# Last pair pass of an attention and expert kernel: second product as seven block products of scaled float16 parts

## The chip, the cores and the metric

The kernel runs on one core of a Trainium2 chip. The metric is the device time of one execution in microseconds (us); the time of a kernel is the median of its runs. The engines are named as in the profile: PE (TensorE, matmuls), PEld (its weight loads), DVE (VectorE), ACT (ScalarE), POOL (GpSimd) and SP (SyncE, which issues every DMA of this kernel).

## The reference

The input is attention (4 batches, 8 heads, 768 positions, 64 features a head) and four experts that every token passes through. Cut to what matters:

```python
# attention: each query sees its neighbours within 16 positions and 24 block summaries
scores_all = concat([where(|i - j| < 16, scale * q @ k.T, -1e9), scale * q @ k_sum.T + log(32)])
a = softmax(scores_all)                        # k_sum: max over blocks of 32
x = a @ concat([v, v_sum])                     # v_sum: mean over blocks of 32; 3072 tokens x 512
# four experts, all of them for every token
p = domain_probs / (domain_probs.sum(-1) + 1e-9)
out = sum over e of p[:, e] * (relu(x @ w1[e]) @ w2[e])   # w1: 512 x 1024, w2: 1024 x 512
```

## The kernel before

The 3072 tokens are eight blocks of 384 (TB, three tiles of 128 tokens each). Attention is done in pieces of 96 queries (`psc` scores, `ms` masked scores, `aw` weights, `awT` the weights turned by a DMA, `px` the values). It feeds the experts, and its pieces stand between the expert products by a table of due times (`steps`, lines 915 to 940, called from `advance`).

The plan of the experts (line 955) has three first passes over single blocks and then three **pair passes** (`PAIRS`, line 778). Pair pass 1 does blocks 2 and 3, pass 2 blocks 4 and 5, pass 3 blocks 6 and 7, each with all four experts, in the orders (3, 2, 1, 0), (0, 1, 2, 3) and (3, 2, 1, 0). Attention is finished in the course of pass 2.

An expert in a pair pass (`pair_units`, lines 857 to 912) has two products. The **first product**, relu(x @ w1), takes the 1024 hidden features in four blocks i of 256. For a pair of token blocks this is a product of 2x2 blocks, and it is made with seven block products in place of eight (`SEVEN`, line 851; `m` counts them from 0): sums and differences of blocks of x and w1 are multiplied into PSUM banks `pha` to `phd`. ACT copies bank a to b after m = 0 and bank d to a buffer `p5` after m = 1; DVE adds these to make banks c (after m = 2) and d (after m = 4). Values are kept as two parts, a rounded one (hi) and the rest (lo), both of type fp32r, and each product is hi·hi + hi·lo + lo·hi: per block i there are 7 x 6 matmuls of 128x384. `to_h` (line 747) makes the hidden values from PSUM: relu and rounding on ACT (`hh`), the rest on DVE (`hl`).

The **second product**, h @ w2, is `mm2` (lines 752 to 776), called by `second` (line 799): per token tile 8 feature blocks x 3 matmuls of 128x512 into a bank `po`, which DVE multiplies by the expert's share `pw` of each token and adds to `acc` (lines 770 to 773). After the fourth expert `acc` goes out. `w2` in two parts is made once and kept in memory (`wd`); later passes load it again, 512 KB for each of 8 feature blocks (`weights`, line 683). The operands of the first product, `w1s` and `w`, are made from `wr` (the raw load of w1 or w2) in the first pass that needs them, by `w1_operands` (line 707), and are loaded again later. `setup_v` (line 168) loads a block of v in four chunks `vch` and makes its means.

What runs when is settled while the program is built: the builder takes instructions in the order of the code, with priorities (RUSH = 200 for the small steps between block products), and an estimate of times places each on its engine's queue. From then on every engine works through its own queue in order, and an instruction waits there for its operands and for buffers to come free. `wr` has 4 buffers, `w1` 14, `w2` 8, `hh` and `hl` 16 each, and PSUM 2 banks `sc`, 2 `av` and 4 `mm`. An instruction recorded by the helper has its line 75, so the profile's rows are told apart by names and shapes.

Of the kernel before, what the change touches and what calls it, by code (L numbers as in the profile page):

```python
# [25 lines left out]
G = 4  # L26
# [36 lines left out]
def attn_moe(ctx: ExitStack, tc: tile.TileContext, qvL, qv0, v0L, kD, kT, vT, w1L, w2L, dpL, cst, out):  # L63
# [82 lines left out]
    def block_stats(ch, dst, hp, op):  # L146
        V.tensor_reduce(dst[:, hp, :], ch.rearrange("p (n k) -> p n k", k=BLK), axis=AX.X, op=op)
# [19 lines left out]

    def setup_v(b):
        vsr = sb.tile([P, G, NB], F32, name=f"vsr{b}", tag="vsr")
        for hp in range(H // 2):  # L170
            ch = chunk(f"vch{b}_{hp}")
            load_chunk(b, hp, ch, vT)
            block_stats(ch, vsr, hp, ALU.add)
        stack_v(b, vsr)

    def stack_v(b, vsr):
        vs5 = sb.tile([P, G, 5, NB], F32, name=f"vs5_{b}", tag="chunk", bufs=CHUNKS)
# [524 lines left out]

    WS = ("11", "s2", "s1", "s3", "12", "s4", "22")

    def w1_operands(e, pr):
        ws = {w: w1_part(f"w1{w}{e}_{pr}") for w in WS}
        if (e, pr) in stored:
            for w in WS:  # L710
                SP.dma_start(ws[w].bitcast(F32), stored[e, pr][w])
            return ws
        r1, r2 = (load_weights(w1L, e, 2 * pr + j, "1") for j in range(2))
        a11, a12 = r1[:, 0:256], r1[:, 256:512]
        a21, a22 = r2[:, 0:256], r2[:, 256:512]
        stored[e, pr] = {}

        def parts(w, raw, lo):
# [33 lines left out]
    def mm2(tb, e, ts, hT, w2):  # L752
        po = {t: ps_mm.tile([P, 512], F32, name=f"po{tb}_{e}_{t}", tag="mm") for t in ts}
        done = 0
        for m, (fc, (whi, wlo)) in enumerate(w2.items()):
            for t in ts:
                hh, hl = (x[:, t * P : (t + 1) * P] for x in hT[tb, fc])
                PE.matmul(po[t], hh, whi, start=m == 0, stop=False)
                PE.matmul(po[t], hh, wlo, start=False, stop=False)
                PE.matmul(po[t], hl, whi, start=False, stop=m == FC - 1)  # L760
                done += 3 * US2
            if m < FC - 1 and (len(ts) > 1 or m in (2, 5)):
                yield done, 1.0
                done = 0
        for t in ts:
            gt = tb * (TB // P) + t
            pe = pw[:, gt, e : e + 1]
            added[gt] = added.get(gt, 0) + 1
            if added[gt] == 1:
                acc[gt] = sb.tile([P, DM], F32, name=f"acc{gt}", tag="acc", bufs=6)  # L770
                V.tensor_scalar_mul(acc[gt], po[t], pe)
            else:
                V.scalar_tensor_tensor(acc[gt], po[t], pe, acc[gt], op0=ALU.mult, op1=ALU.add)
            if added[gt] == E:
                SP.dma_start(out[gt * P : (gt + 1) * P, :], acc.pop(gt))
# [28 lines left out]
        for tb in tbs[len(whole) :]:  # L804
            yield from mm2(tb, e, range(TB // P), hT, w2)

    def with_fetch(units):
        for n, us in enumerate(units):
            if n in (1, 8):
                fetch()  # L810
            yield us

    def plain_units(tbs, e, early=0, last=False):
# [40 lines left out]
        ("b", "s3", "t3"), ("c", "s4", "22"), ("b", "22", "t4"),  # L854
    )

    def pair_units(pr, e, last=False):

        tbs = (2 * pr, 2 * pr + 1)
        xp = xpair[pr]  # L860
        hT = {}
        _, w2 = kept.pop(e, ({}, {}))
        kept.clear()
        order = orders[pr, e]
        for n, i in enumerate(order):
            fetch((pr, e, i))
# [10 lines left out]
            for m, (k, w, x) in enumerate(SEVEN):  # L877
# [11 lines left out]
                if m == 0:  # L889
                    A.copy(new("b"), o)  # L890
                elif m == 1:
                    five = sb.tile([P, TB], F32, name=f"p5{pr}_{e}_{i}", tag="hs", bufs=2)
# [10 lines left out]
                else:  # L903
                    to_h(hT, tbs[0], e, f2, o)
                ahead_of.close()
                if m == 3:
                    for fc in (f1, f2):
                        if fc not in w2:
                            w2[fc] = weights(w2L, e, fc, "2", PL)
                yield 6 * US1, SLOW  # L910
        kept[e] = {}, w2
        yield from with_fetch(second(tbs, e, hT, w2, last))


    steps = []
# [130 lines left out]
```

## Time and profile before

| | us |
|---|---|
| median of 3 runs | 1179.01 (1178.67 to 1179.54) |
| the profiled execution | 1176.52 |
| its span | 1174.7 |
| PE busy in 0 to 276 (first passes) | 262.37 of 276 |
| DVE busy in 0 to 276 | 186.56 of 276 |

The profile comes from one execution, whose own time is 1176.52; the span is the time from the first to the last recorded instruction in it. Busy times are sums over the instructions of one engine. PSUM and weight traffic apart, an engine of the five that is idle while PE is busy costs nothing, so the profile is read from PE's side: where PE waits, for whom, and what that engine did just before.

### The profile page before, as it was taken

Reading aid. Unit: us, or ns where it says so; the run is one execution under the profiler, and the core shown is the slowest. Engines: PE = TensorE matmul, PEld = TensorE weight load, DVE = VectorE, ACT = ScalarE, POOL = GpSimd, SP = SyncE. Lnnn points to the kernel's source line nnn. Section 1 sums busy time; section 2 is a strip of 40 time slices with the busy share of each in tenths; the row PEclk is TensorE's granted clock in tenths of the full one; section 3 lists DMA queues with packets and bytes.
Section 4 is the critical chain, followed back from the end, with each engine's and each line's share of the span. In section 5 each row is a group of like instructions: output and inputs, shape, how many; then the busy total and the mean of one; then the engine's idle time right before and its main releaser. Section 6 shows DMA issues by size and latency. Waiting matters only on the chain.

```text
span 1174.7 us, 20612 instructions
## 1 busy us (share of the span) xinstructions
PE 1150.5 (98%) x7188; PEld 1021.0 (87%) x7188; DVE 631.4 (54%) x1519; ACT 541.2 (46%) x1586; POOL 468.5 (40%) x578
## 2 busy tenths in 40 slices
PE   9898899999979999999999999999999999999998
PEld 7787789998968989898898989889898998989896
DVE  6778775555796837558586543535354222323131
ACT  5678667655666736546375443434343211202020
POOL 2398677846786737547265122221202000000000
PEclk9999999999999999999999999999999999999999
DMA  6699787957996878789963859678571556566531
GB/s 240 227 281 321 225 250 218 305 118 215 307 251 182 272 228 263 225 277 288 320 196 102 255 149 289 202 213 284 141 205 61 159 156 212 165 197 189 163 98 54
DMA packets 202329, 249.66 MB, mean 213 GB/s; under 512 B 82672, under 2 KB 118512, under 8 KB 202224
## 3 DMA queue, kind: packets, MB, share of 16 engines
q1 hardware_dynamic: 202224, 248.34, 69.6%
q8 instruction: 57, 0.93, 0.3%
q14 instruction: 48, 0.39, 0.1%
HBM read 174.22 MB, written 57.15 MB: 197 GB/s over the span
## 4 chain that ended last, share of the span: by engine, by line
PE 85%; DMA 4%; DVE 4%; POOL 3%; ACT 2%; issue 1%; SPq 1%; POOLq 0%; DVEq 0%; ACTq 0%
PE po L75 42%; PE phb L75 13%; PE pha L75 9%; PE ph L75 5%; PE phd L75 4%; PE phc L75 4%; PE psc L75 4%; PE px L75 3%; DMA vch<-in_vT 1%; PE pav L75 1%; DMA wr<-in_w2L 1%; DMA kch<-in_kT 1%; DVE ms L75 1%; SPq L75 1%; ACT ms L75 1%
## 5 line engine op out<-in xcount | busy, mean ns | idle before, releaser
L75 PE MATMUL po<-w,hh 128*128 128x512 f32 x1536 | 480.5, 394 | 0.0
L75 PEld LDWEIGHTS po<-w,hh 128*128 128x128 f32 x1536 | 284.2, 188 | 61.0
L75 PE MATMUL po<-w,hl 128*128 128x512 f32 x768 | 302.8, 397 | 0.0
L75 PEld LDWEIGHTS po<-w,hl 128*128 128x128 f32 x768 | 144.4, 188 | 31.5
L75 POOL TENSOR_TENSOR ks<-kr,ks 128x304 fp32r<-128x304 f32 x112 | 99.7, 897 | 176.8 <-ACT ks L75 160.5
L75 DVE CUSTOM_DVE_ANT_0 ms<-psc,c_sb 96x152 f32<-96x152 f32 x256 | 69.2, 306 | 104.6 <-PE psc L75 103.4
L75 PE MATMUL phb<-xh_t,w1s 128*128 128x384 f32 x384 | 114.2, 338 | 0.1
L75 ACT ACTIVATE ms<-ms,nb 96x152 f32<-96x152 f32 x256 | 104.3, 415 | 16.5 <-DVE nb L75 15.6
L75 PE MATMUL pha<-xh,w 128*128 128x384 f32 x384 | 110.7, 335 | 0.0
L75 DVE SCALAR_TENSOR_TENSOR acc<-po,pw,acc 128x512 f32<-128x512 f32 x72 | 51.9, 746 | 108.8 <-PE po L75 108.8
L75 PE MATMUL ph<-xh,wh 128*128 128x384 f32 x256 | 88.0, 347 | 4.8 <-ACT wh L75 3.7
L75 PE MATMUL ph<-xl,wh 128*128 128x384 f32 x256 | 87.4, 341 | 2.3 <-DVE xl L75 2.3
L75 DVE TENSOR_TENSOR aw<-ms,aw 96x512 f16<-96x512 f32 x112 | 77.2, 723 | 21.5 <-ACT aw L75 21.3
L75 PE MATMUL ph<-xh,wl 128*128 128x384 f32 x256 | 87.1, 341 | 1.2 <-POOL wl L75 1.2
L75 ACT CAST ks<-kr 128x304 fp32r<-128x304 f32 x112 | 48.1, 445 | 80.4 <-PE psc L75 62.9
L75 POOL TENSOR_TENSOR wl<-wr,wh 128x512 fp32r<-128x512 f32 x44 | 62.6, 1425 | 45.0 <-ACT wh L75 44.9
L75 ACT CAST aw<-ms 96x512 f16<-96x512 f32 x112 | 53.3, 523 | 56.3 <-issue 37.8
L75 POOL TENSOR_TENSOR qv<-qv,v 128x256 f32<-128x256 f32 x56 | 40.8, 739 | 78.2 <-ACT v L75 78.0
L75 ACT CAST v<-qv 128x256 bf16<-128x256 f32 x112 | 44.5, 405 | 59.2 <-PE px L75 40.8
L75 PEld LDWEIGHTS phb<-xh_t,w1s 128*128 128x128 f32 x384 | 70.8, 188 | 1.0 <-ACT phb L75 0.2
L75 PEld LDWEIGHTS pha<-xh,w 128*128 128x128 f32 x384 | 70.5, 188 | 0.3
L75 PE MATMUL phb<-xl_t,w1s 128*128 128x384 f32 x192 | 64.3, 335 | 0.0
(122 smaller groups left out, 2169.3 us busy)
## 6 DMA issues: line engine op xcount, KB each, us to landing
w<-wd SPq DMA_DIRECT2D x80, 512.0 KB, 4.4
w1s<-wds SPq DMA_DIRECT2D x112, 256.0 KB, 3.5
w<-wd SPq DMA_DIRECT2D x84, 256.0 KB, 3.4
wr<-in_w1L SPq DMA_DIRECT2D x76, 256.0 KB, 4.3
qv<-in_qvL SPq DMA_DIRECT2D x56, 320.0 KB, 4.4
wd<-w SPq DMA_DIRECT2D x32, 512.0 KB, 4.3
wds<-w1s SPq DMA_DIRECT2D x64, 256.0 KB, 2.7
kr<-in_kD SPq DMA_DIRECT2D x56, 256.0 KB, 3.7
```

Of the source, the lines that this page charges most:

```text
L75: ins = getattr(self.engine, name)(*a, **kw)
```

## The change

In pair pass 3 (`SCALED`) the second product is made in the same way as the first: with seven block products, over a pair of token tiles (blocks 6 and 7) and the halves of w2's features and columns. Its operands are float16 in two parts. So that they fit float16, w2, w1 and v are scaled by powers of two that come from their largest absolute values.

- **Maxima.** `scan` (called from `w1_operands` and, in pair pass 1, from `pair_units`) reduces each raw part of w1 and w2 on DVE to one column (`found`), 64 reductions of 128x512 in all; `setup_v` adds four of 128x768 for v's block 3. When an expert's sixteen maxima are there, `over_partitions` stores them to memory, loads all of them to every partition (`ve`, `w3e`, `w2e`, `w1e`, `w0e`) and reduces again; `scales` makes the powers of two in a few small DVE steps.
- **Operands of w2.** `make_w2` makes one block i of one expert: two loads of 256 KB, four casts on ACT, four rests on DVE, four sums on POOL and four stores. It is called from pass 2 on (`MAKE`). Pass 3 then loads 512 and 384 KB for each block (`w2_operands`).
- **Hidden values.** `to_seven` makes relu on ACT into memory, sums and differences on DVE, and float16 parts by casts on ACT and rests on DVE.
- **Second product.** `second_seven`: per token tile 7 block products x 4 blocks i x 3 matmuls of 128x256. `add_up` adds each finished bank, half a tile wide, with the shares in `pm`.

```diff
+    def scan(e, which, fc, part):
...
+        V.tensor_reduce(
+            t[:, which, fc : fc + 1], part, axis=AX.X, op=ALU.max, apply_absolute_value=True
+        )
+        if len(seen) == 2 * FC:
...
+            V.tensor_reduce(m, t, axis=AX.X, op=ALU.max)
+            over_partitions(m, 2, f"w{e}")
+            w_scale[e] = s, inv = scales(m, 2, f"w{e}")
...
+    def over_partitions(m, k, name):
+        room = dram.tile([P, k], F32, name=f"{name}d")
+        SP.dma_start(room, m)
+        every = sb.tile([P, P, k], F32, name=f"{name}e", tag="hs", bufs=2)
...
+        SP.dma_start(every.rearrange("p q k -> p (q k)"), flat.broadcast_to([P, P * k]))
+        V.tensor_reduce(m, every.rearrange("p q k -> p k q"), axis=AX.X, op=ALU.max)
...
+    def make_w2():
...
+        r1, r2 = (load_weights(w2L, e, 2 * i + j, "2s") for j in range(2))
...
+        def parts(k, n, raw):
...
+            A.activation(t[:, 0], raw, AF.Copy, scale=s)
+            V.scalar_tensor_tensor(t[:, 1], raw, s, t[:, 0], op0=ALU.mult, op1=ALU.subtract)
...
+            SP.dma_start(room if k < 3 else room.rearrange("p (v f) -> p v f", v=2), t)
...
+    def to_seven(hs, e, i, m, src, ahead_of):
...
+        A.activation({3: h11, 4: h22, 5: h21, 6: h12}[m], src, AF.Relu, scale=s)
...
+            A.copy(hi, raw)
+            V.tensor_tensor(lo, raw, hi, op=ALU.subtract)
...
+        if m == 4:
+            split(("11", "22"), ra)
+        elif m == 5:
+            V.tensor_tensor(h22, h21, h22, op=ALU.add)
+            V.tensor_tensor(h21, h11, h21, op=ALU.subtract)
+            V.tensor_tensor(h11, h22, h11, op=ALU.subtract)
+            split(("s2", "s1"), ra)
+            split(("s3",), h21)
+        elif m == 6:
+            split(("12",), h12)
+            V.tensor_tensor(h12, h12, h11, op=ALU.subtract)
+            split(("s4",), h12)
...
+    def second_seven(pr, e, order, hs, w2):
...
+                    todo += [(ah, bh), (ah, bl), (al, bh)]
+                for j, (l, r) in enumerate(todo):
+                    PE.matmul(
+                        o, l, r, start=j == 0 and m < 2, stop=j == len(todo) - 1, skip_group_check=m >= 2
+                    )
+                with tc.high_priority(offset=RUSH):
+                    if m == 0:
+                        A.copy(new("b"), o)
...
+                        A.copy(five, o)
+                    elif m == 2:
+                        V.tensor_tensor(new("c"), o, five, op=ALU.add)
+                    elif m == 4:
+                        V.tensor_tensor(bank["d"], o, five, op=ALU.add)
...
         kept[e] = {}, w2
-        yield from with_fetch(second(tbs, e, hT, w2, last))
+        if seven:
+            units = second_seven(pr, e, order, hs, w2)
+        else:
+            units = second(tbs, e, hT, w2, last)
+        yield from with_fetch(units, MAKE.get((pr, e), ()))
```

The queues show where the new instructions stand. First DVE in pair pass 1, at the start of expert 0's first product (`phc1_0_0` is bank c of its block 0; `psc48`, `ms48` and `nb48` are attention piece 48, `b12_3` and `v0_3` the means of v's block 3, `acc9` to `acc11` the sums of expert 1's last tiles). Before:

```order
L75 SCALAR_TENSOR_TENSOR acc10_6169<-po3_1_1_7800,pw_73,acc10_6169 128x512
L75 SCALAR_TENSOR_TENSOR acc11_6171<-po3_1_2_7801,pw_73,acc11_6171 128x512
L75 CAST b12_3_7898<-v0_3_7896 120x512
L75 TENSOR_SCALAR b12_3_7898<-b12_3_7898,c_sb_72 120x512
L75 ISA ms48_8011,nb48_8012<-psc48_0_8014,c_sb_72 96x152
L75 ISA nb48_8012 96x1
L75 ISA ms48_8011,nb48_8012<-psc48_0_8014,c_sb_72 96x152
L75 ISA nb48_8012 96x1
L75 TENSOR_TENSOR v0_3_7896<-v0_3_7896,b12_3_7898 120x512
L75 TENSOR_TENSOR w1220_2_8136<-wr10_5_8139,w1220_2_8136 128x256
L75 SCALAR_TENSOR_TENSOR b12_3_7898<-b12_3_7898,c_sb_72 120x512
L75 TENSOR_TENSOR phc1_0_0_8051<-phb1_0_0_8034,p51_0_0_8043 128x384
```

Of the changed kernel, from the reduction of v's maxima over the partitions (`ve`) on:

```order
L79 TENSOR_REDUCE found_74<-ve_8006 128x1
L79 TENSOR_REDUCE found_74<-w20_5_8442 128x1
L79 SCALAR_TENSOR_TENSOR acc11_6205<-po3_1_2_7893,pw_73,acc11_6205 128x512
L79 ISA ms48_8118,nb48_8119<-psc48_0_8121,c_sb_72 96x152
L79 TENSOR_TENSOR v0_3_7992<-v0_3_7992,b12_3_7994 120x512
L79 ISA ms48_8118,nb48_8119<-psc48_0_8121,c_sb_72 96x152
L79 TENSOR_SCALAR found_74<-found_74 128x1
L79 TENSOR_REDUCE found_74<-w20_6_8578 128x1
L79 TENSOR_TENSOR w1220_2_8245<-wr10_5_8248,w1220_2_8245 128x256
L79 TENSOR_REDUCE found_74<-w20_7_8580 128x1
L79 SCALAR_TENSOR_TENSOR b12_3_7994<-b12_3_7994,c_sb_72 120x512
L79 TENSOR_SCALAR found_74<-found_74 128x1
```

`phc1_0_0` is the next row. Ahead of it stand three maxima of w2, the reduction of `ve`, which needs two transfers after v's last maximum, and small steps; the two rows `nb48`, each behind its `ms48`, are left out here.

Second, ACT at the end of expert 2's first product in pair pass 3. Before, the last rows of that product are the relus of its block 3:

```order
L75 ACTIVATE hh6_2_6_12699<-pha3_2_3_12667 128x384
L75 COPY p53_1_0_12938<-phd3_1_0_12931 128x384
L75 ACTIVATE hh7_2_7_12714<-phd3_2_3_12676 128x384
L75 ACTIVATE hh7_2_6_12724<-phc3_2_3_12691 128x384
L75 ACTIVATE hh6_2_7_12734<-phb3_2_3_12674 128x384
```

And of the changed kernel (`hr`, `hk`, `hq` hold relu in memory; `hh2_311` is the cast of h11 and h22 of block 3, `hs42_2` that of block 2's s4; `poa`, `pob`, `pod` are banks of the second product):

```order
L79 ACTIVATE hk2_3_13438<-phc3_2_3_13429,found_74 128x384
L79 ACTIVATE hq2_3_13439<-phb3_2_3_13412,found_74 128x384
L79 CAST hs42_2_13402<-hq2_2_13356 128x384
L79 CAST hh2_311_13453<-hr2_3_13437 128x768
L79 COPY pob2_0_13501<-poa2_0_13488 128x256
L79 CAST hh2_3s2_13467<-hr2_3_13437 128x768
L79 CAST h122_3_13481<-hq2_3_13439 128x384
L79 CAST hs32_3_13471<-hk2_3_13438 128x384
L79 COPY p62_0_13516<-pod2_0_13503 128x256
L79 COPY p62_1_13653<-pod2_1_13640 128x256
L79 COPY pob2_1_13638<-poa2_1_13625 128x256
```

Between the last relu and the first copy of the second product there are now two casts, and four further rows between the first copy and the copies of `pod`.

Third, PE at the same place, where the second product asks for `hh2_311`:

```order
L79 MATMUL poa2_0_13488<-w2s2_33_13443,hh2_311_13453 128x256
L79 LDWEIGHTS hh2_311_13453
L79 MATMUL poa2_0_13488<-w2s2_33_13443,hh2_311_13453 128x256
L79 LDWEIGHTS hh2_311_13453
L79 MATMUL poa2_1_13625<-w2s2_33_13443,hh2_311_13453 128x256
L79 LDWEIGHTS hh2_311_13453
L79 MATMUL poa2_1_13625<-w2s2_33_13443,hh2_311_13453 128x256
L79 LDWEIGHTS hl2_311_13454
L79 MATMUL poa2_0_13488<-w2s2_33_13443,hl2_311_13454 128x256
L79 LDWEIGHTS hl2_311_13454
L79 MATMUL poa2_1_13625<-w2s2_33_13443,hl2_311_13454 128x256
L79 LDWEIGHTS hh2_0s2_13190
```

Here stood matmuls of 128x512 into one bank `po6_2_0` with `hh6_2_6` and `hl6_2_6`. Now two tiles' banks alternate, four matmuls on the rounded part and two on the rest; the next matmul goes into `pob2_0`, the bank that ACT's copy fills. Thirteen matmuls with operands of blocks 0 to 2 stand ahead of these rows, behind the last `phb3_2_3`.

More of the change, by code (lines that the diff above doesn't have):

```diff
@@ L716, in w1_operands @@
         stored[e, pr] = {}
+        scan(e, 0, 2 * pr, r1)
+        scan(e, 0, 2 * pr + 1, r2)
         def parts(w, raw, lo):
@@ new lines, in w2_operands @@
+    def w2_operands(e, i):
+        t = []
+        for n, d in zip((4, 3), made[e, i]):
+            t.append(sb.tile([P, n, 512], F16, name=f"w2s{e}_{i}{n}", tag="w2", bufs=FC))
+            SP.dma_start(t[-1], d)
+        ws = {}
+        for k, names in enumerate((("21", "22"), ("t1", "t3"), ("t4", "t2"))):
+            for o, w in enumerate(names):
+                ws[w] = tuple(
+                    t[k // 2][:, 2 * (k % 2) + v, 256 * o : 256 * (o + 1)] for v in range(2)
+                )
+        ws["11"] = tuple(t[1][:, 2, 256 * v : 256 * (v + 1)] for v in range(2))
+        return ws
@@ new lines, in attn_moe, with mixed @@
+    mix, h_scale = {}, {}
+    def mixed(e):
+        gts = range(2 * SCALED * (TB // P), 2 * (SCALED + 1) * (TB // P))
+        if not mix:
+            t = sb.tile([P, len(gts), E], F32, name="pm", tag="ksr")
+            for k, gt in enumerate(gts):
+                mix[gt] = t[:, k]
+            mix["all"] = t
+        s, inv = w_scale[e]
+        h_scale[e] = facts(2)
+        hs, back = h_scale[e][:, 0:1], h_scale[e][:, 1:2]
+        V.tensor_tensor(hs, v_scale[SCALED][0], s[:, 0:1], op=ALU.mult)
+        V.tensor_tensor(back, v_scale[SCALED][1], inv[:, 0:1], op=ALU.mult)
+        V.tensor_scalar(
+            mix["all"][:, :, e : e + 1], pw[:, gts[0] : gts[-1] + 1, e : e + 1], back, inv[:, 1:2],
+            op0=ALU.mult, op1=ALU.mult,
+        )
@@ L765, in mm2, with add_up @@
         for t in ts:
[L766 to L775, printed above, removed]
-        yield done, 1.0
-    PAIRS = ((1, (3, 2, 1, 0)), (2, (0, 1, 2, 3)), (3, (3, 2, 1, 0)))
+            add_up(tb * (TB // P) + t, e, po[t])
+        yield done, 1.0
+    def add_up(gt, e, po, c0=0):
+        pe = (mix[gt] if gt in mix else pw[:, gt])[:, e : e + 1]
+        cols = po.shape[-1]
+        if gt not in acc:
+            acc[gt] = sb.tile([P, DM], F32, name=f"acc{gt}", tag="acc", bufs=6)
+        part = acc[gt][:, c0 : c0 + cols]
+        if added.get(gt, 0) < DM:
+            V.tensor_scalar_mul(part, po, pe)
+        else:
+            V.scalar_tensor_tensor(part, po, pe, part, op0=ALU.mult, op1=ALU.add)
+        added[gt] = added.get(gt, 0) + cols
+        if added[gt] == E * DM:
+            SP.dma_start(out[gt * P : (gt + 1) * P, :], acc.pop(gt))
     orders, todo, ready = {}, [], {}
@@ L888, in pair_units @@
                 ahead_of.enter_context(tc.high_priority(offset=RUSH))
-                if m == 0:
+                if seven and m >= 3:
+                    if m == 4:
+                        V.tensor_tensor(bank["d"], o, five, op=ALU.add)
+                    to_seven(hs, e, i, m, bank["adcb"[m - 3]], ahead_of)
+                elif m == 0:
                     A.copy(new("b"), o)
@@ L905, in pair_units @@
                 ahead_of.close()
-                if m == 3:
+                if m == 3 and seven:
+                    w2[i] = w2_operands(e, i)
+                elif m == 3:
                     for fc in (f1, f2):
```

119 lines of the change are left out of this document (117 added, 2 removed).

## The prediction

> **What bounds the kernel now.** First the page, then the time by stages, then what TensorE waits for. On the page the columns are busy time, share of the span and instructions of each engine, and below that the chain that ended last:
>
> ```profile
> PE 1150.5 (98%) x7188; PEld 1021.0 (87%) x7188; DVE 631.4 (54%) x1519; ACT 541.2 (46%) x1586; POOL 468.5 (40%) x578
> PE 85%; DMA 4%; DVE 4%; POOL 3%; ACT 2%; issue 1%; SPq 1%; POOLq 0%; DVEq 0%; ACTq 0%
> ```
>
> TensorE is busy for 98% of the span and carries 85% of the chain. The stages (length, busy time of PE, PEld, DVE, ACT, POOL, then the granted clock, the DMA share and GB/s; 374 to 651 is pair pass 1, to 921 pass 2, to 1171 pass 3):
>
> ```profile
> 276.00:374.00 98.00, 91.13 (x598) 80.75 (x597) 76.88 (x172) 60.41 (x187) 74.21 (x84) 0.97 0.87 254
> 374.00:651.00 277.00, 276.94 (x1758) 244.68 (x1757) 178.85 (x418) 152.21 (x469) 159.49 (x206) 1.00 0.77 240
> 651.00:921.00 270.00, 270.00 (x1681) 240.22 (x1680) 119.95 (x305) 105.94 (x311) 54.57 (x78) 1.00 0.65 194
> 921.00:1171.00 250.00, 250.00 (x1250) 224.73 (x1248) 68.45 (x121) 43.63 (x96) 0.00 (x0) 1.00 0.52 162
> ```
>
> In the three pair passes TensorE never stops, so a matmul less is time less and a wait more is time more, one for one. All its long waits lie earlier; the list of waits of TensorE (total, times, longest) begins with the first row below, and the last two lines are what it does around the longest:
>
> ```profile
> PE px L75 <- DMA awT<-aw: 9.4, 4, 5.6
> PE ph L75 <- DVE xl L75: 2.3, 1, 2.3
> ...
> 349.95 0.61 PE L75 MATMUL px<-awT,v 128*64 128x96 f16 x10 [5.55 <-DMA awT<-aw]
> ```
>
> **The change, part by part,** against the profiled run (1176.5 us; span 1174.7). The median of the three runs is 1179.0, so I add 2.5 at the end.
>
> **1. Matmuls of the last pass.** Groups by shape in 921 to 1175 us, and some starts on the timeline:
>
> ```profile
> L75 PE MATMUL po<-w,hh 128*128 128x512 f32 x385 | 119.3, 391 | 0.0
> ...
> 1149.61 0.62 PE L75 MATMUL po<-w,hh 128*128 128x512 f32 x2
> ...
> 1150.30 0.39 PE L75 MATMUL po<-w,hh 128*128 128x512 f32 x1
> ...
> 7.55 1.47 PE L75 MATMUL pz<-z 128*128 128x512 bf16 x7
> L75 PE MATMUL pz<-z 128*128 128x384 bf16 x4 | 0.8, 326 | 0.0
> L75 PEld LDWEIGHTS <-z 128*128 128x128 bf16 x7 | 0.6, 97 | 0.5
> ```
>
> The mean of 391 ns counts overlapping neighbours; the starts count: three matmuls between 1149.61 and 1150.30, so 0.69 / 3 = 0.229 us each. Gone are 576 (4 experts x 2 blocks x 3 x 8 x 3): 131.9 us. They become 4 x 3 x 7 x 4 x 3 = 1008 matmuls of 256 columns in float16. No such row exists. The nearest is the seven bfloat16 matmuls at 7.55 (three of 512 and four of 384 columns, 3072 in all): the last ends one latency after its start, so 1.47 − 0.33 = 1.14 us is the spacing of the first six, 2688 columns if the last is a 384: 0.425 ns a column, 109 ns for 256. The other bound is the float16 row quoted above at its full clock, ten of 96 columns:
>
> ```profile
> 343.97 0.38 PE L75 MATMUL px<-awT,v 128*64 128x96 f16 x10
> 344.19 0.21 PE L75 MATMUL px<-awT,vs 120*64 120x96 f16 x2
> ```
>
> The next row starts 0.22 us later, 44 ns a pair if the two halves (128*64) run side by side, 0.46 ns a column: 117 ns. I take 109, whole-array matmuls like the new ones: 109.9 us. **Term 1: 109.9 − 131.9 = −22.0** (−14.0 at 117).
>
> The page "TensorE: Matmul & The Clock Gate" of the Trainium skill, Part 3, section "The mechanism", says that a weight load overlaps running matmuls only where the row groups differ. By that rule each of the 1008 loads would stand beside its matmul: at 97 ns (the row above) that is 97.8 us more, a term 1 of +75.8 and a total of 1272. The last pass does not bear it out: PEld is busy for 224.7 of 250.0 us there while PE never stops. I give it 0.01, inside the case of 117 ns below.
>
> **2. The seam between first and second product, four times.** Before, TensorE meets no wait there. The second product now needs, of the last block, relu into memory, a float16 cast of two blocks at once (hh..11), its rest on DVE (hl..11), and then ACT's copy poa to pob. The rows that price them (groups of 651 to 1175):
>
> ```profile
> L75 ACT ACTIVATE hh<-phb 128x384 fp32r<-128x384 f32 x32 | 15.7, 490 | 70.8 <-PE phb L75 70.8
> L75 ACT COPY p<-phd 128x384 f32<-128x384 f32 x32 | 15.4, 482 | 29.9 <-PE phd L75 29.8
> L75 ACT CAST aw<-ms 96x512 f16<-96x512 f32 x12 | 7.4, 619 | 14.3 <-issue 13.4 <-DVE ms L75 0.9
> L75 DVE SCALAR_TENSOR_TENSOR hl<-phd,hh 128x384 fp32r<-128x384 f32 x32 | 17.8, 556 | 13.3 <-ACT hh L75 13.2
> ```
>
> From 482 ns at 384 elements to 619 at 512, about 1 ns an element: 0.75 to 0.88 us for 768; DVE's rest of 768 is about 1.0 by 556 for 384. Take expert 2, in the order shown in the change. After the last phb of the first product TensorE still has 13 matmuls whose operands exist, 13 x 0.109 = 1.4 us. ACT meanwhile: relu of h12 0.5, cast hs4 of block 2 0.4 (back to back), cast hh2_311 0.8, so 1.8: TensorE waits 0.4. After four more matmuls (2.2) it wants hl2_311, ready at 1.8 + 1.0: waits 0.6. After two more, pob2_0 needs the copy of poa2_0: 0.4. Then 18 matmuls whose operands come in time, 8 of the last block, and pob2_1 finds ACT behind two casts and two copies: 0.7. Sum 2.1. Experts 1 and 0 have the same order; expert 3 has one cast more ahead of each copy, 3.3. With 0.4 for 1.8 MB of new w2 parts landing just then, 3 x 2.1 + 3.3 + 0.4 = **+10.0**. Bounds: 4 (only the two waits for the last block's parts stay) and 20 (each operation twice as long). The first product hides the rest: per block of 7.3 us (42 matmuls at 0.173, the 384-column spacing of this pass) ACT has about 5 to 6 us and DVE 6 to 7.
>
> **3. The tail.** The last eviction halves:
>
> ```profile
> 1171.06 0.75 DVE L75 SCALAR_TENSOR_TENSOR acc<-po,pw,acc 128x512 f32<-128x512 f32 x1 [4.79 <-PE po L75]
> ```
>
> **−0.3** (not under −0.4, nor over 0).
>
> **4. Maxima in the earlier passes.** 64 DVE reductions of 128x512 and four of 128x768 come into stages where DVE is the fullest helper. Its rows and windows:
>
> ```profile
> 571.63 0.95 DVE L75 TENSOR_REDUCE vsr<-vch 128x24 f32<-128x768 f32 x1
> ...
> 574.67 0.95 DVE L75 TENSOR_REDUCE vsr<-vch 128x24 f32<-128x768 f32 x1 [1.86 <-DMA vch<-in_vT]
> ...
> 586.62 0.57 DVE L75 TENSOR_TENSOR phc<-phb,p 128x384 f32<-128x384 f32 x1
> 310.90:342.40 31.50, 30.18 (x246) 27.01 (x245) 28.89 (x64) 23.38 (x78) 29.60 (x35) 1.00 0.96 265
> 565.00:588.00 23.00, 23.00 (x141) 19.74 (x139) 14.30 (x34) 9.77 (x30) 7.75 (x10) 1.00 0.93 319
> ks<-ksr SPq DMA_DIRECT2D x16, 24.0 KB, 3.9
> ```
>
> A reduction of 512 is 0.95 x 512 / 768 = 0.63 us.
> - Before px at 349.95: 2.6 of the 31.5 us were free and seven reductions (4.4 us) come in, 1.8 late; aw now stands behind one acc (0.7), some xl rows behind it (−0.5): the 5.55 us wait grows by **+2.0** (0 to 5).
> - At phc1_0_0 (order in the change): the last vch is reduced at 575.5 and its maximum at 577.5; then two small transfers follow each other, 3.9 us each by the nearest row (ks), so ve lands at 585.3. DVE stands still at its reduction, and behind it are three scans (1.9), acc (0.7), two ms (0.5), v0 (0.8), w1220 (0.4), b12 (0.7), small ones (0.6): 5.6, so phc starts at 590.9 in place of 586.6. TensorE wants it written at 587.8 (next phb) and it ended at 587.2: of 4.3, **+3.7** (0 to 5).
>
> ```profile
> 587.78 0.38 PE L75 MATMUL phb<-xh_t,w1s 128*128 128x384 f32 x1
> 512.20 0.32 SPq L75 DMA_DIRECT2D w<-wd  x1
> w<-wd SPq DMA_DIRECT2D x80, 512.0 KB, 4.4
> 520.70 0.33 PE L75 MATMUL phb<-xh_t,w1s 128*128 128x384 f32 x1
> ```
>
> - At phc1_1_0: the scan of w21_7 waits for its load, issued at 512.2, there at 516.6; behind it 3.9 us of rows (scan, rs, ms, w, aw) and phc (0.55) end at 521.1, wanted at 520.7: **+0.4** (0 to 3).
> - The other three round trips, the scan of w22_7 and the 16 makings of w2 (all stand in pass 2 in the order; ACT there has 164 us free, DVE 150): **+1.4** (0 to 4).
>
> The new DMAs of pass 2 (32 loads of 256 KB and stores of 14 MB) meet a share of 0.65: nothing. Term 4: **+7.5** (0 to 17).
>
> **Sum:** −22.0 + 10.0 − 0.3 + 7.5 = −4.8, so 1171.7 for the profiled run, **1174.2** on the scale of the median.
>
> **Rivals.**
> - **Hidden seams and maxima.** For it: ACT is busy for 43.6 of 250 us in the last pass and DVE for 68.5, so queues may run ahead of my walk; the reductions need 44 us and DVE had 98 free in pass 1. Against it: the windows above are full where it counts. Seams 5, maxima 2: −22.0 + 5 − 0.3 + 2 = −15.3, **1163.7**.
> - **DVE's queue takes the gain and the clock with it (slower).** The place is pass 1 and the stage before it: a reduction that waits for a transfer holds phc, hl and aw behind it. In the trace a TensorE stop of 2.3 us was followed by a lower clock:
>
> ```profile
> 134.24 0.44 PE L75 MATMUL ph<-xl,wh 128*128 128x384 f32 x1 [2.30 <-DVE xl L75]
> 134.00:140.00 6.00, 5.76 (x24) 5.76 (x25) 4.56 (x9) 3.22 (x12) 3.88 (x5) 0.72 1.05 365
> ```
>
> At 0.72 over 6 us a stop costs 1.7 more. With term 4 at 17 and two such stops (3.4): −22.0 + 10.0 − 0.3 + 20.4 = +8.1, **1187.1**. It is slower than before once term 4 passes 12.3. The same page of the Trainium skill, Part 1, section "What's actually happening", puts the lowering of the clock after an idle window of about 3.4 us; by that rule the two stops cost no clock, and this rival would be 1183.7. The trace disagrees: 2.30 us were enough.
> - **Float16 matmuls at 117 ns** (0.46 ns a column): +8.0 on the forecast, **1182.2**. Against it: the seven whole-array ones.
> - That the change does not do what it says: the order shows the sums of w2 all in pass 2, none in pass 3, and 1008 narrow matmuls; nothing is left for this.
>
> **How the numbers follow.** Forecast 0.36 (its own range 1171 to 1178), hidden 0.29, DVE's queue 0.25, 117 ns 0.10. A measurement of this kernel tells about 0.2% (2.4 us) from no change: faster is under 1176.7, slower above 1181.4. The forecast puts 0.26 on faster and 0.10 on same; hidden 0.29 on faster; DVE's queue 0.05 on same and 0.20 on slower; 117 ns 0.04 and 0.06. So faster 0.55, same 0.19, slower 0.26. The range, 1161 to 1188, takes in all four and leaves 0.2 out at the ends of terms 2 and 4.
>
> **What would show it.** Term 1: starts of po rows 109 ns apart. Term 2: TensorE waits on ACT hh, DVE hl and ACT pob at four places, some 0.4 to 0.7 each. Term 4: the px wait near 350 at 7.5 us, phc late near 588 with DVE waiting for ve, and clocks under 0.9 only near 134 and 350. The prediction is wrong if the seams show no waits, if the reductions take much over 0.63, or if a stage before 921 grows by over 12 us.

## The result, and the profile after

The changed kernel takes 1198.24 us (median of 4 runs, 1192.71 to 1199.33) against 1179.28 on the same chip: ratio 1.0152, 95% interval 1.012 to 1.0184. It is slower by 1.5%, where a gain of 0.4% was forecast; the time lies 10 us above the range.

Top of the page of the changed kernel, then its stages as before (length, busy time of PE, PEld, DVE, ACT, POOL, granted clock, DMA share, GB/s):

```profile
PE 1142.4 (95%) x7620; PEld 1013.5 (85%) x7620; DVE 790.8 (66%) x1834; ACT 634.9 (53%) x1754; POOL 527.0 (44%) x642
```

```profile
276.00:374.00 98.00, 91.65 (x596) 80.71 (x595) 83.59 (x185) 59.31 (x184) 72.92 (x85) 0.97 0.84 252
374.00:651.00 277.00, 261.06 (x1654) 231.39 (x1653) 199.60 (x492) 145.12 (x441) 150.94 (x194) 0.98 0.81 237
651.00:921.00 270.00, 263.16 (x1636) 233.88 (x1635) 166.72 (x373) 141.99 (x384) 114.90 (x143) 0.99 0.86 270
921.00:1171.00 250.00, 241.77 (x1644) 217.85 (x1643) 144.06 (x258) 106.65 (x217) 11.63 (x16) 0.99 0.53 182
```

In 374 to 921 us TensorE used to be busy without a break; now it is idle for 15.9 + 6.8 us there, and slowed after the long stops: its clock is lower in these stages. What it waits for between 374 and 930 us (total, times, longest):

```profile
PE psc L79 <- DVE nb L79: 9.5, 1, 9.5
PE phb L79 <- DVE phc L79: 4.4, 3, 2.0
PE phb L79 <- ACT phb L79: 3.2, 3, 1.5
PE pha L79 <- DVE nb L79: 1.9, 1, 1.9
PE phd L79 <- DMA w1s<-wds: 1.6, 1, 1.6
```

And from 930 us on, in the last pass:

```profile
PE poa L79 <- ACT hh L79: 3.8, 4, 2.3
PE pob L79 <- ACT pob L79: 2.9, 7, 0.5
PE poa L79 <- DVE hl L79: 1.5, 4, 0.4
PE poa L79 <- DVE acc L79: 0.6, 1, 0.6
```

So the last pass went nearly as forecast: 8.8 us of waits at the seams, where term 2 had 10.0, on the engines it named. The parts differ from the forecast, which had 0.4 us for each wait for `hh`: the first seam alone has 2.35 us, and the clock is lower behind it (second row, 989.0 to 993.4 us, 0.61). In a timeline row, the bracket is the idle time before it and what ended it:

```profile
988.68 0.61 PE L79 MATMUL poa<-w2s,hh 128*128 128x256 f16 x4 [2.35 <-ACT hh L79]
```

```profile
989.00:993.40 4.40, 3.79 (x20) 2.34 (x19) 3.40 (x6) 2.01 (x4) 0.00 (x0) 0.61 0.02 4
```

The matmuls of the last pass (timeline of TensorE):

```profile
999.93 1.47 PE L79 MATMUL poc<-w2s,hs 128*128 128x256 f16 x12
1001.24 1.25 PE L79 MATMUL poa<-w2s,h 128*128 128x256 f16 x10
```

Twelve in 1.31 us are 0.109 us each, the 109 ns of term 1. The loss lies in the passes before. The longest stop, TensorE's row first:

```profile
604.41 0.92 PE L79 MATMUL psc<-ks,qs 128*96 128x152 f32 x4 [9.46 <-DVE nb L79]
```

DVE ahead of it:

```profile
590.28 0.42 DVE L79 CAST b<-v 120x512 bf16<-120x512 f32 x1
598.65 0.69 DVE L79 TENSOR_REDUCE found<-w 128x1 f32<-128x512 f32 x1 [7.95 <-DMA w<-wd]
...
601.76 0.28 DVE L79 TENSOR_REDUCE found<-ve 128x1 f32<-128x128 f32 x1
```

And the DMA queue (SPq, SyncE's) ahead of that, first as issued, then by stretches of 2 us, then the store's time from issue to landing:

```profile
586.21 0.32 SPq L79 DMA_DIRECT2D vd<-found  x1
586.62 0.86 SPq L79 DMA_DIRECT2D w<-wd  x2
594.23 0.32 SPq L79 DMA_DIRECT2D ve<-vd  x1
```

```profile
588.00:590.00 2.00, 2.00 (x13) 1.72 (x13) 1.78 (x3) 1.33 (x3) 0.00 (x0) 1.00 2.07 219
590.00:592.00 2.00, 2.00 (x13) 2.00 (x12) 0.70 (x3) 1.37 (x5) 1.18 (x2) 1.00 0.88 31
592.00:594.00 2.00, 2.00 (x14) 2.00 (x13) 0.00 (x0) 0.65 (x2) 0.43 (x1) 1.00 0.90 39
```

```profile
vd<-found SPq DMA_DIRECT2D x1, 0.5 KB, 8.0
```

Followed back: the matmuls of the scores of attention piece 48 wait for DVE, DVE stands 8 us at a maximum of w2 whose load is out, and that load was issued right behind `vd`, the store of v's 128 maxima of 4 bytes. The store takes 8.0 us. For part of them the DMA engines count as 88 to 90% busy and move 31 to 39 GB/s. DVE reaches the reduction of `ve`, for which the prediction had it wait, only afterwards, and does not wait there.

What the place costs shows from the last matmul into `pha` ahead of the scores to the sixth into `phc` behind them, the same matmuls in both kernels, before and after, and from the clock behind the stop:

```profile
587.28 0.34 PE L75 MATMUL pha<-xh,w 128*128 128x384 f32 x1
...
589.74 0.33 PE L75 MATMUL phc<-xh,w1s 128*128 128x384 f32 x1
```

```profile
594.61 0.34 PE L79 MATMUL pha<-xh,w 128*128 128x384 f32 x1
...
610.93 0.34 PE L79 MATMUL phc<-xh,w1s 128*128 128x384 f32 x1
```

```profile
605.00:610.00 5.00, 3.04 (x11) 2.83 (x10) 4.90 (x17) 2.54 (x9) 4.42 (x5) 0.50 0.22 69
```

That is 16.3 us in place of 2.5, so 13.9 more: two stops (9.46, and 1.96 for `phc`) and matmuls at a granted clock of 0.50.

### The profile page after: what moved, and what is told of

It is laid out like the page before. It is cut to its first block, busy times and chain, and to the rows that moved or that the text cites. A ratio compares the mean times of both kernels' runs of the same rounds, so it can differ in the third digit from the quotient of the medians.

```text
span 1197.6 us, 22374 instructions
## 1 busy us (share of the span) xinstructions
PE 1142.4 (95%) x7620; PEld 1013.5 (85%) x7620; DVE 790.8 (66%) x1834; ACT 634.9 (53%) x1754; POOL 527.0 (44%) x642
## 4 chain that ended last, share of the span: by engine, by line
PE 40%; DMA 4%; DVE 3%; ACT 2%; issue 1%; POOL 1%; SPq 0%; POOLq 0%; ACTq 0%; DVEq 0%
PE po L79 12%; PE phb L79 8%; PE pha L79 5%; PE pob L79 4%; PE phc L79 3%; PE phd L79 2%; PE poa L79 2%; DMA w<-wd 1%; PE poc L79 1%; DMA wr2s<-in_w2L 1%; PE px L79 1%; PE pod L79 1%; PE psc L79 1%; DVE hl L79 1%; POOL wr2s L79 1%
## 5 line engine op out<-in xcount | busy, mean ns | idle before, releaser
L79 PE MATMUL po<-w,hh 128*128 128x512 f32 x1152 | 364.3, 397 | 1.7 <-DVE hl L79 1.7
L79 PEld LDWEIGHTS po<-w,hh 128*128 128x128 f32 x1152 | 213.8, 190 | 47.7 <-DVE hl L79 2.0
L79 PE MATMUL po<-w,hl 128*128 128x512 f32 x576 | 228.1, 398 | 0.0
L79 PEld LDWEIGHTS po<-w,hl 128*128 128x128 f32 x576 | 108.8, 189 | 23.8
L79 PE MATMUL phb<-xh_t,w1s 128*128 128x384 f32 x384 | 117.5, 347 | 7.6 <-DVE phc L79 4.4
L79 DVE SCALAR_TENSOR_TENSOR wp<-wr2s,found,wp 128x512 f16<-128x512 f32 (+1 forms) x64 | 50.8, 795 | 45.2 <-ACT wp L79 40.0
L79 ACT ACTIVATE wp<-wr2s,found 128x512 f16<-128x512 f32 (+1 forms) x64 | 42.5, 667 | 53.1 <-DMA wr2s<-in_w2L 19.9
L79 PEld LDWEIGHTS psc<-ks,qs 128*96 128x96 f32 x448 | 53.3, 165 | 18.1 <-DVE nb L79 9.8
L79 PE MATMUL psc<-ks,qs 128*96 128x152 f32 x448 | 57.0, 251 | 10.5 <-DVE nb L79 9.5
```

Source lines behind the costliest of these rows:

```text
L79: ins = getattr(self.engine, name)(*a, **kw)
```

## The experiments

A note on their weight first. Single runs of these kernels spread by up to 12 us, and two of the programs below turned out to be the same (see the third group): they measured 1.0135 and 1.0070 on two chips. So between groups a difference under 0.7% tells nothing, and the TensorE idle time of the profiled executions, by stage, is read beside it. In the table "idle 1" is 277.00 less PE's busy time in 374 to 651 us, "idle 2" 270.00 less that in 651 to 921. The range is the interval of the ratio to the kernel before on the same chip. Each program has one profiled execution, which can lie some us from its median. By the traces, those two equal programs and the twins of the fourth group have the same order of instructions on every engine. Other edits move more than they name: 379 of the 7620 matmuls stand elsewhere in the constants kernel than in the changed one.

| kernel | ratio (interval) | idle 1 | idle 2 |
|---|---|---|---|
| changed, again | 1.0160 (1.0136 to 1.0185) | 14.2 | 9.0 |
| constants, no round trips | 1.0135 (1.0113 to 1.0156) | 7.0 | 7.8 |
| no maxima | 1.0049 (1.0034 to 1.0064) | 1.2 | 8.2 |
| round trips as turns | 1.0148 (1.0133 to 1.0164) | 8.0 | 9.0 |
| no making | 0.9928 (0.9906 to 0.9951) | 0.8 | 0.0 |
| making: transfers alone | 0.9971 (0.9953 to 0.9989) | 0.6 | 2.0 |
| no maxima, casts on POOL | 0.9968 (0.9948 to 0.9988) | 1.3 | 2.1 |
| maxima of a ready tile | 1.0432 (1.0397 to 1.0467) | 6.1 | 7.3 |
| constants, w2's maxima late | 1.0070 (1.0048 to 1.0092) | 7.6 | 5.2 |
| the same, casts on POOL | 1.0035 (1.0014 to 1.0057) | 6.4 | 2.8 |
| nothing left out, late, POOL | 1.0183 (1.0146 to 1.0219) | 13.4 | 7.6 |
| the same with turns | 1.0132 (1.0102 to 1.0162) | 9.9 | 6.8 |
| constants, no maxima of w2 | 1.0089 (1.0071 to 1.0107) | 1.4 | 11.0 |
| constants, no maxima of w1 | 1.0104 (1.0077 to 1.0131) | 6.8 | 8.1 |
| constants, maxima of 32 columns | 1.0081 (1.0060 to 1.0103) | 4.2 | 7.4 |
| constants and one store, waited for | 1.0166 (1.0139 to 1.0193) | 15.7 | 6.7 |
| constants and one store, 4 bytes | 1.0166 (1.0147 to 1.0185) | 12.6 | 11.8 |
| constants and one store, 64 bytes | 1.0125 (1.0106 to 1.0144) | 8.6 | 11.9 |

### First group: round trips or reductions

The changed kernel once more:

> The changed kernel once more, unaltered, for a second profile. If the 9.5 us stop of TensorE near 594 us comes from the order of the queues (the maxima of v stored in 4-byte elements, the loads of w2 behind them on the DMA queue, DVE waiting for one of these loads), it is there again, 6 to 12 us long, and the time is 1192 to 1200. If it was an accident of one execution, it is gone or under 4 us in this profile and the profiled execution is 6 to 10 us shorter than 1199.

The stop is there again, 8.4 us, so it comes from the program.

Constants in place of the round trips:

```diff
     def over_partitions(m, k, name):
-        room = dram.tile([P, k], F32, name=f"{name}d")
...
+        V.memset(m, 0.5 if name == "v" else 0.1)
```

> Leaves out the reductions over the partitions: each maximum is set to a constant after its own reduction, so the five stores, five loads and their waits are gone, while all 68 reductions of weights and v stay. Theory ROUND TRIPS (the stores and loads of single elements hold up the DMA queue and DVE): some 14 us at the 594 us stop and 2 to 4 elsewhere go, so 1179 to 1183. Theory REDUCTIONS (DVE time of the 68 maxima and their waits for loads): only 1 to 4 us go, 1194 to 1197.

1192.04 us: 4 less than the changed kernel on the same chip, between both theories and nearer to REDUCTIONS. The long stop is gone from the profile (idle 1 falls from 14.2 to 7.0), the median hardly follows. But the profiled execution took 1184.83 us, 13.8 less than that of the changed kernel (1198.61); the other three took 1190 to 1194, and no profile shows why.

Without the reductions too (those of `scan` and of `setup_v`):

```diff
-        V.tensor_reduce(
-            t[:, which, fc : fc + 1], part, axis=AX.X, op=ALU.max, apply_absolute_value=True
-        )
...
-            V.tensor_reduce(m, t, axis=AX.X, op=ALU.max)
```

> Leaves out the 68 reductions as well as the five round trips; the scales are constants. What is left of the change is the making of w2's sums in pass 2 and the last pass itself. ROUND TRIPS: 1 to 4 us below the kernel that leaves out the round trips alone. REDUCTIONS: 12 to 20 us below that kernel. In both cases the last pass gains 12 to 13 us by terms 1 to 3 of the prediction, so 1166 plus what the making of w2's sums costs in pass 2: 1167 to 1168 if that is the 1 us forecast, 1172 to 1176 if pass 2 loses the 5 to 8 us seen in the profile of the changed kernel by the making itself.

1182.83 us, 9 less: between the two, nearer to the 12 to 20 of REDUCTIONS. But this kernel, with no maxima left, is still slower than the one before, so neither theory holds the whole. Idle 1 is nearly nothing and idle 2 stands at 8.2. Something in pass 2 costs by itself.

The maximum over the partitions by turns on DVE:

```diff
+        V.tensor_copy(a[:, 0:k], m)
+        V.transpose(b, a)
+        V.tensor_reduce(m[:, 0:1], b, axis=AX.X, op=ALU.max)
...
```

> Makes the maximum over the partitions on DVE, with two 32x32 turns and some ten small steps (about 1 to 2 us of DVE each time, five times), in place of a store and a load. All reductions stay and the result is the full one. ROUND TRIPS: 1 to 4 us above the kernel with constants, 1180 to 1186. REDUCTIONS: no better than the changed kernel, 1193 to 1200.

1194.50 us, against ROUND TRIPS: the long stop is gone here too, but the time is only 1.7 under the changed kernel's 1196.20.

### Second group: the making of w2's sums

Fifteen of the sixteen makings left out, the last pass unchanged:

```diff
-    to_make = [(e, i) for e in PAIRS[-1][1] for i in range(FC // 2)]
+    to_make = [(PAIRS[-1][1][0], 0)]
...
-        for n, d in zip((4, 3), made[e, i]):
+        for n, d in zip((4, 3), made[PAIRS[-1][1][0], 0]):
```

> Leaves out the maxima, the round trips and 15 of the 16 makings of w2's sums (the last pass loads the one that is made in place of each); the last pass has the same instructions as in the changed kernel. Theory LAST PASS GAINS (terms 1 to 3 as forecast, the loss lies in the preparation): 12 to 13 us under the kernel before, ratio 0.988 to 0.991. Rival: the last pass itself gains less than 6 us, then the ratio is 0.995 or more.

Ratio 0.9928, 8.5 us of 1178: the last pass gains, less than the 12 to 13 expected. Against the kernel without maxima this is 1.2%, some 14 us, more than the chips differ. So making costs more than the last pass brings: some 14 us against 8.5, though the 14 is taken across chips and carries their 0.65%.

The transfers of the makings alone:

```diff
+        if made:
+            for n, raw in ((256, r1[:, 0:256]), (512, r2), (512, r1), (512, r2)):
+                SP.dma_start(dram.tile([P, n], F32, name=f"mv{e}_{i}{len(moved)}"), raw)
...
+            return
```

> As the one before, but the two loads and four stores of each of the 15 makings stay, without casts, rests and sums. Theory TRANSFERS (the makings cost by their DMA traffic, which delays other loads): 8 to 15 us above the kernel without makings, near the kernel without maxima (1182.8). Theory ENGINES (the casts and rests stand in the queues of ACT and DVE and wait for their loads there): within 3 us of the kernel without makings.

Ratio 0.9971: 5 us over the kernel without makings on the same chip, between ENGINES and TRANSFERS. Loads in pass 2 (651 to 921 us, the median to landing last) are slower with the transfers than without; first the kernel without makings, then this one:

```profile
w1s<-wds SPq DMA_DIRECT2D x56, 256.0 KB, 3.8
```

```profile
w1s<-wds SPq DMA_DIRECT2D x56, 256.0 KB, 4.9
```

The casts on POOL:

```diff
-            A.activation(t[:, 0], raw, AF.Copy, scale=s)
+            PL.tensor_scalar_mul(t[:, 0], raw, s)
```

> The kernel without maxima and round trips, its 64 casts of w2's sums made by POOL in place of ACT; rests stay on DVE, all transfers stay. ENGINES with ACT as the place (TensorE waits of 3.1, 1.0 and 0.4 us for ACT's copy phb in pass 2): those waits go and the time is 4 to 8 us under 1182.8. TRANSFERS: no change within 2 us. If DVE's rests now wait for a slower POOL and hold hl and phc, it is slower than 1182.8.

ENGINES, with ACT as the place: 1173.81 us, ratio 0.9968, 9 under the kernel with the casts on ACT (on another chip; 4 to 8 were expected), and idle 2 falls from 8.2 to 2.1, what the transfers alone leave. It is faster than the kernel before, but it leaves the maxima out. The place shows in the profile of the kernel without maxima, ACT first, then TensorE:

```profile
658.73 0.72 ACT L79 ACTIVATE wp<-wr2s,found 128x512 f16<-128x512 f32 x1 [1.54 <-DMA wr2s<-in_w2L]
659.35 0.47 ACT L79 COPY phb<-pha 128x384 f32<-128x384 f32 x1
```

```profile
659.88 0.69 PE L79 MATMUL phb<-xh_t,w1s 128*128 128x384 f32 x1 [3.06 <-ACT phb L79]
660.36 0.52 PE L79 MATMUL phb<-xl_t,w1s 128*128 128x384 f32 x1
660.68 0.52 PE L79 MATMUL phb<-xh_t,w1s 128*128 128x384 f32 x1
```

A cast of w2 (`wp`, the float16 part, from `wr2s`, the raw load or a sum made of it) stands ahead of the copy that TensorE needs and waits for its load; ACT is idle, and the copy stands behind it. Over all makings (groups by shape of the changed kernel, ACT, 600 to 930 us; the last part is idle time before them):

```profile
L79 ACT ACTIVATE wp<-wr2s,found 128x512 f16<-128x512 f32 x46 | 33.2, 721 | 39.6 <-POOL wr2s L79 19.4 <-DMA wr2s<-in_w2L 9.2 <-DMA ws<-wp 5.1
L79 ACT ACTIVATE wp<-wr2s,found 128x256 f16<-128x256 f32 x16 | 8.1, 507 | 13.5 <-DMA wr2s<-in_w2L 10.7 <-issue 2.8
```

The 62 casts work for 41 us, and ACT is idle ahead of them for 53 more: 19.9 until a load had landed, 19.4 until POOL had made a sum, the rest for others.

Reductions of a tile that is always there, beside the constants:

```diff
-            t[:, which, fc : fc + 1], part, axis=AX.X, op=ALU.max, apply_absolute_value=True
+            t[:, which, fc : fc + 1], c_sb[:, 0:512], axis=AX.X, op=ALU.max, apply_absolute_value=True
```

> The kernel with constant scales and all 68 reductions, but each reads a tile that is always there (the constants, 512 columns, in place of the weights and v). Theory WAITS (a reduction costs because it stands in DVE's queue and waits for its load): about 9 us under 1192.0, like the kernel without reductions (1183). Theory DVE TIME (43 us more of DVE's own time): 1189 to 1193.

1229.27 us, outside both theories: with nothing to wait for, all 68 reductions moved to the start of DVE's queue, and attention of the first block, which needs DVE, stood behind them. It decides nothing between WAITS and DVE TIME, but prices them (groups of DVE, 0 to 110 us):

```profile
L79 DVE TENSOR_REDUCE found<-c_sb 128x1 f32<-128x512 f32 x68 | 41.4, 669 | 1.2 <-DMA c_sb<-in_cst 1.2
```

### Third group: the place of w2's maxima

The call of `scan` for w2 was put into the second product of its expert:

```diff
-                if m in (4, 5) and pr == PAIRS[0][0]:
-                    fc = (f1, f2)[m - 4]
-                    scan(e, 1, fc, w2[fc][0].bitcast(F32))
...
+            if n in late:
+                scan(e, 1, late[n], w2[late[n]][0].bitcast(F32))
```

> Constant scales, all 68 reductions of the real data, but the 32 of w2 come in the second product of their expert, when each part has long been loaded, in place of the first product right behind the loads. Theory WAITS (the reductions cost by standing in DVE's queue in the first product, for a load or ahead of phc): 4 to 7 us under 1192.0, so 1185 to 1188. Theory DVE TIME: within 2 us of 1192.0.

1185.97 us is what WAITS expected, and it shows nothing: the order of DVE's and every other queue is the same as without the edit. Here the place of the call in the code did not set the place in the queue. So this is the second measurement of one program, and its 0.65% from the first is the error to be kept in mind. The 14 runs of the two together have a median of 1186.4 us, 11 under the 1197.5 of the changed kernel's eight runs, and 4 over the kernel without maxima.

The same with the casts on POOL, as above:

> The same with the casts of w2's sums on POOL. If the two costs are separate (casts 9 us, reductions of w2 4 to 7), they add up: 1176 to 1179, about the kernel before. If the casts' gain was only another place for the same wait, it stays above 1183.

1181.01 us, 5 under its twin on the same chip; idle 2 falls from 5.2 to 2.8. That lies between the two expectations: the casts' gain is there beside the reductions, and smaller than the 9 above.

With the true maxima and their round trips back in it:

> The changed kernel with its round trips and real maxima, the 32 reductions of w2 in the second product and the casts on POOL; nothing is left out. The round trips add what they added before (about 4 us): 1180 to 1184. If the stop near 594 us needed the reductions of w2 behind the store (theory QUEUE: loads of w2 held on the DMA queue behind a load that waits for the store, DVE behind them), it is under 3 us now.

1198.47 us, with no gain over the changed kernel. The stop is there, 7.8 us, as the reductions of w2 had not moved. The round trips had been given 4 us, and 1180 to 1184 was expected: between this pair they cost 17.

And with turns on DVE, as in the first group, in place of the round trips:

> The same with the maximum over the partitions made by turns on DVE in place of stores and loads; nothing is left out. Between the kernel with constants and the one with round trips: 1177 to 1182.

1193.68 us, over the range expected. Turns save 5 us of the 17 here; the rest stays open.

### Fourth group: which reductions, and the store

Both are the constants kernel with `scan` reducing only w1 (shown) or only w2 (`which == 1`):

```diff
+        if which == 0:
+            V.tensor_reduce(
...
```

> The kernel with constant scales, without the 32 reductions of w2 (those of w1 and v stay). It was 1192.0 with all reductions and 1182.8 with none. If the reductions that wait for w2's loads are what costs: 1183 to 1186. If w1's are: 1189 to 1192.

> The same without the 32 reductions of w1 (those of w2 and v stay). If w2's reductions cost: 1189 to 1192. If w1's do (they stand between the steps that make the parts of w1 in the first product, where DVE is fullest): 1183 to 1186.

1186.66 and 1189.87 us; with 1.0070 and 1.0135 for the kernel that has both, the times do not tell them apart. The profiles, one of each, do: without w2's reductions idle 1 falls from 7.0 to 1.4, without w1's to 6.8. The stops of pass 1 are w2's. But idle 2 of the first is 11.0: part of what pass 1 saves is lost in pass 2, where ACT's casts hold the queue (one wait of 5.9 us for the copy phb).

```diff
-            t[:, which, fc : fc + 1], part, axis=AX.X, op=ALU.max, apply_absolute_value=True
+            t[:, which, fc : fc + 1], part[:, 0:32], axis=AX.X, op=ALU.max, apply_absolute_value=True
```

Above, `scan` reduces the first 32 columns of each part.

> The kernel with constant scales and all 68 reductions at nearly the same places of DVE's queue and behind the same loads, but each reads only 32 columns, the rest is left out: about 0.1 us in place of 0.66. Theory WAITS: as with whole reductions, 1189 to 1193. Theory DVE TIME: most of the 9.2 us goes, 1182 to 1186.

1185.69 us lies with DVE TIME by its words, with the same doubt about the kernel it is set against. Idle 1 is 4.2, between 7.0 and 1.2: by these single profiles about half of the stops is DVE's own time, half the waits for loads.

One store in front of the loads:

```diff
+        if name == "v":
+            SP.dma_start(dram.tile([P, k], F32, name=f"{name}d"), m)
         V.memset(m, 0.5 if name == "v" else 0.1)
```

> The kernel with constant scales, plus one store: v's 128 maxima, 4 bytes a partition, go to memory in front of the loads of w2's parts 4 and 5; nothing loads them and nothing waits for them. Theory STORE (the store of single elements holds the DMA queues): packets of 4096 bytes take over 5 us behind it, the load of part 4 takes over 10 us, DVE waits 6 to 8 us for it and TensorE 6 to 9 us. Theory ROUND TRIP (the wait of the second transfer for the first holds the queue): no such packets, the load lands in 4 to 7 us and TensorE waits under 3 us there.

STORE: TensorE waits 9.2 us at the same place, the store lands after 8.6 us. One thing is not as the words say: the memset on DVE writes what the store reads and waited 5.3 us for it. So two more, from a copy, with the same order on all engines, 4 against 64 bytes a partition:

```diff
-            wide = sb.tile([P, 1], F32, name=f"{name}e", tag="hs", bufs=2)
-            V.tensor_copy(wide, m)
+            wide = sb.tile([P, 16], F32, name=f"{name}e", tag="hs", bufs=2)
+            V.tensor_copy(wide, m.broadcast_to([P, 16]))
...
```

> The kernel with constant scales, plus one store of v's 128 maxima, 4 bytes a partition, made from a copy so that no instruction waits for it; it stands between the loads of w2's parts 4 and 5 on the DMA queue, and the order on all engines is that of its twin with 64 bytes. Theory STORE (single elements hold up what is issued behind them): a load of 512 KB behind the store lands after 10 us or more and TensorE waits 4 to 9 us before 606 us; the time is 3 to 7 us above its twin. Rival: the stop came from waiting for the store; then both twins agree within 2 us, and nothing is late.

> The twin: the same store with 64 bytes a partition (16 copies of the maximum). Theory STORE with the size as its cause: the store lands in 2 to 4 us, loads behind it in 4 to 7 us, TensorE waits under 4 us in all before 606 us, the time is that of the kernel without a store (ratio to the kernel before about 1.013). If any store at this place does it, it is as slow as its twin.

DMA issues of the kernel with 4 bytes in 578 to 606 us (KB each, median us from issue to landing), then its TensorE timeline at the stop:

```profile
w<-wd SPq DMA_DIRECT2D x3, 512.0 KB, 12.5
vd<-ve SPq DMA_DIRECT2D x1, 0.5 KB, 8.0
```

```profile
594.65 0.92 PE L79 MATMUL psc<-ks,qs 128*96 128x152 f32 x4 [6.89 <-DVE nb L79]
```

The same two views of the kernel with 64 bytes, the issues in 588 to 592 us, so that here too all three loads stand behind the store:

```profile
w<-wd SPq DMA_DIRECT2D x3, 512.0 KB, 6.9
vd<-ve SPq DMA_DIRECT2D x1, 8.0 KB, 3.0
```

```profile
597.49 0.57 PE L79 MATMUL psc<-ks,qs 128*96 128x152 f32 x4 [0.80 <-DVE nb L79]
```

STORE, with the size of the element as its cause: nothing waits for either store, only the loads behind the one with 4 bytes are late. 1197.00 against 1193.22 us, on one chip. (The profiled execution with 64 bytes is a long one, 1198.60 us; it was idle for 16.2 us in its first 276 us against 12.2 of its twin, ahead of the store.)

No version with real maxima beats the kernel before. The page "DMA: Bandwidth & Descriptors" of the Trainium skill, in the table at its head, gives 512 bytes as the least size for full rate and says that below it the engine reads, changes and writes back. Both stores of the twins are under that size, and the one with 64 bytes a partition cost almost nothing here: between 4 and 64 lies the difference that counted. No run shows what happens inside a store.

## Why the prediction was wrong, by its steps

- **Term 1 (−22.0) was right in its price**: 0.109 us a matmul, weight loads hidden.
- **Term 2 (+10.0) was right in its mechanism and its sum**: 8.8 us of waits, and 9.4 in the kernel without makings, at the casts, the rests and the copies that it named. That the sum came so near is partly luck: the first seam was longer than forecast, the waits for the rests and the copies shorter.
- **Terms 1 to 3 together were a little too good.** −12.3 was forecast, and the kernel without maxima and makings but one measured −8.5 (interval −11.1 to −5.8). Two things that the terms had left out show in the last pass. The clock is lower behind the first seam (above). And the first product's first matmul behind a float16 block is followed by the next after 0.26 us in place of 0.17, at 16 places between 1000 and 1160 us, some 1.4 us (timeline of the changed kernel; the starts count):

```profile
1011.42 0.42 PE L79 MATMUL pha<-xh,w 128*128 128x384 f32 x1
1011.68 0.34 PE L79 MATMUL pha<-xl,w 128*128 128x384 f32 x1
1011.85 0.51 PE L79 MATMUL pha<-xh,w 128*128 128x384 f32 x2
```

- **Term 4 is the step that failed.** It gave +7.5 and at most 17 for the whole preparation. From −8.5 to +18.8 (the changed kernel measured again) it is some 27 us: by the medians some 14 for the makings, 4 for the reductions and 11 for the round trips, the split uncertain by the 0.65% above. Two of its lines were far too small, and the clock had none.
- First, "the 16 makings of w2 (all stand in pass 2 in the order; ACT there has 164 us free, DVE 150)", part of +1.4, and the sentence that new DMAs "meet a share of 0.65: nothing". The makings cost some 14 us. Free time of an engine was taken for cover. But in ACT's queue a cast that waits for a load or for POOL's sum keeps the copy behind it from TensorE while ACT is idle: with the casts on POOL the time fell by 5 us on one chip and by 9 across two. And the transfers alone lengthened other loads from 3.8 to 4.9 us and cost about 5.
- Second, "+3.7" at phc1_0_0. It was 13.9 there. The two transfers were priced at 3.9 us each by the nearest row; the store took 8.0 and held up a load behind it to 12 us. The working did not have that: it had DVE wait for `ve`, and it began at `ve`, while the maximum of w2 that waited stands ahead of it in DVE's queue. The store is worth 4 us by the twins; all round trips are worth 4 to 17 by pairs of programs and 11 by all runs, which the experiments do not take apart further.
- The clock: TensorE is busy for 1142.4 us in the changed kernel and, with the same 7620 matmuls, for 1132.6 in the kernel without makings (first line of its page below). These 9.8 us are part of the 32.7 between the two spans; the mean granted clock was 0.984 against 0.994. Term 4 priced stops at their length alone; only the slower rival had a price for the clock, 3.4 us.

```profile
PE 1132.6 (97%) x7620; PEld 1007.3 (86%) x7620; DVE 710.2 (61%) x1701; ACT 600.3 (52%) x1694; POOL 473.6 (41%) x582
```

- "+2.0" at px did not come: TensorE is idle for 6.9 us in 276 to 374 us before, and for 6.4 after.
- The reductions of 0.67 us were priced rightly (0.63), and their sites named: `phc` in pass 1 (4.4 us of waits) and w2's. Their cost is 2 to 10 us, by two measurements of one program.
- **The rival that was slower** named the right kind of mechanism, a queue held by an instruction that waits, and the right point: term 4 over 12.3. It put all of it on DVE in pass 1 and the stage before; about half lies in pass 2, on ACT and in the transfers of the makings, which no rival had. Its clock loss came too. The px wait near 350, its first sign, did not grow: the longest wait for `awT` was 5.6 us and is 4.7.

## What to carry to other kernels

An engine's free time does not hide an instruction that waits in its queue: what counts is what stands behind it, and moving such work to another engine can pay (here ACT's casts to POOL, though a cast takes longer there: 1.65 against 0.72 us). A stop of TensorE can cost more than its length, since the clock was lower behind the long ones. Before a small side task is put on a shared DMA queue, ask which loads are issued behind it, who waits for them, and how small its elements are. And where a builder orders the queues, read the order after an edit: putting the call elsewhere in the code moved nothing.

## What the runs showed of the hardware

- A store of 128 elements of 4 bytes took 8.0 us, and the three loads of 512 KB behind it landed after 12.5 us (median); with 128 elements of 64 bytes it took 3.0 and they 6.9.
- After a TensorE stop of 3.06 us (profile of the kernel without maxima, above) matmuls of 384 columns started 0.32 us apart (660.36 to 660.68) in place of 0.173, and the granted clock was 0.50 from 660 to 665 us; behind the stop of 9.46 us it was 0.50 from 605 to 610. The page "TensorE: Matmul & The Clock Gate" of the Trainium skill, Part 1, section "What's actually happening", has this after an idle window of about 3.4 us; here, as with the 2.30 us of the prediction, a shorter stop was enough.
- Behind a block of float16 matmuls, the first fp32r matmul of 384 columns was followed by the next after 0.26 us (1011.42 to 1011.68) in place of 0.17. No run here shows the cause.
- The same program measured 0.65% apart on two chips against the same kernel before, with intervals of 0.2% each.
